# Idle matmuls over a 128-column block, and the queries of pairs 0 and 1 loaded in 1536-byte pieces

## The chip, the cores and the metric

One Trainium2 chip, one NeuronCore. The time is the device time of one execution in microseconds; the kernel before was run three times, and once more with the hardware profiler on.

## The reference

Inputs q, k, v have the shape (4 batches, 8 heads, 768 positions, 64) in float32; the output has the shape (4, 768, 512).

```python
k_chunks = k.reshape(B, H, nc, chunk, D)                    # chunks of 32 keys, nc = 24
k_min, k_max = np.min(k_chunks, axis=3), np.max(k_chunks, axis=3)
ub = np.sum(np.maximum(q[:, :, :, None, :] * k_min[:, :, None], q[:, :, :, None, :] * k_max[:, :, None]), axis=-1)
ub = np.where(causal, ub, -1e9)                             # an upper bound for each query and chunk
top_chunks = np.argsort(ub, axis=-1)[..., -6:]              # the 6 best chunks of each query
scores = scale * np.matmul(q, k.transpose(0, 1, 3, 2))      # masked: selected chunks, and not the future
attn = exp(scores - max) / (sum + 1e-9)
x = np.matmul(attn, v)                                      # heads side by side: (4, 768, 512)
h = gelu(x @ w_in); u, v = h[..., :512], h[..., 512:]       # gMLP block on the attention's output
v_n = layernorm(v) * g_ln
v_s = einsum('ts,bsd->btd', w_sg, v_n) + b_sg               # mixes positions
out = x + (u * v_s) @ w_out
```

## The kernel before

The 32 heads are worked on in 16 pairs (p, heads i = 0 and 1); pairs 0 to 3 are batch 0, and so on. For each pair:

- `load_rows` loads keys (`kn`) and queries (`qn`), one transfer for each head, and `load_v` the values. For pairs below 8 a transfer puts query 128 j + p of a head on partition p, in six pieces of 64 numbers (256 bytes).
- `kside` transposes the keys on TensorE into PSUM (`ktr`, two halves of 384 positions), takes the minimum and maximum of each chunk from there on VectorE (`kmm`, L615), and copies the keys as bf16 into `KA` (`kev`, L433 on ScalarE or L434 on VectorE). `wsub` (GpSimd, L632) subtracts the minimum from the maximum.
- `qside` transposes the queries (`qtr`): for pairs 0 to 3 in three 128x128 float32 transposes for each half of 384 positions (`rows_T`, L520; both heads at once, 64 partitions of the result each), for pairs 4 to 7 in twelve transposes of 64 rows (`rows_T2`, L530). `qev` (L433 or L434) copies each half to `qT`; `rel` makes the positive part `rT` (GpSimd L655 or VectorE L657); `qcast` makes bf16 copies `QA`.
- `select` (pairs 0 to 3) computes the bounds on TensorE (`ub`, L691) from `W`, `qT` and `rT`, and VectorE ranks them: `utr` (transpose), `m8` (nine searches for the eight largest), `dn` and `dt` (the mask `Dt`).
- `scores` computes scores into PSUM and adds the mask by matmuls (`sc`, L852 and L858); ScalarE exponentiates (`exp`, L867; L818 from pair 4 on); GpSimd cuts the diagonal; `head` multiplies by the values (`pv`, `pvd`, L890 and L897) and VectorE divides (`rcp`, `xs`).
- After a batch's four pairs, `xtrans` transposes the result (`xtr`, copied by `xev`, L434), and `moe_h` and `moe_g` compute the block: `hv` (L940), GELU and squares on ScalarE (`gv` L945, `sq` L951), `nmu` (minus the mean, L948 or L950), `rstd` (GpSimd L970), `vhat` (the normalised values: VectorE L974 or GpSimd L980), `hu` (L989) with `gu` (L994), the mixing `pt` (L1006), `vs` (L1016), `gt`, the output product `ou` (L1030) with `os` (L1039) and the stores.

`xtrans` of batch 1 ends with three copies on VectorE, and every `hv` of batch 1 waits for all four transposed tiles.

The program is a list of operations. `TABLE` was written by a planner: the order of the operations on each engine, the PSUM slot of each tile (`slots`), and which operations run on their other engine (`alt`; a `qev`, `kev` or `wbe`, for one, may run on ScalarE or VectorE). Each engine runs its list strictly in this order; an operation waits for the semaphores of what it reads and of the last user of its PSUM slot. The transfers are issued in the order of the list of SyncE (`sp`), a few by ScalarE.

PSUM has two large slots for scores (PSC) and four small ones (PSG) of one bank each for everything else.

At the start, ahead of all loads, TensorE runs matmuls whose result nobody reads (`idle`, L376): one at first, eight ahead of the first `ktr` and two ahead of the first `qtr` (`filler` in the table: `53:8 58:2`). Their operand `warm` is cleared by VectorE (L373):

```python
warm = E[1][:, 0, 0:512]
    P.op("dve", lambda d: d.memset(warm, 0.0), dve(512), ("init", 0), writes=["warm"])
    def idle(e):
        return e.matmul(ps_score.aps[1][:, 0:512], warm[:, 0:128], warm, start=True, stop=True, skip_group_check=True)
```

The helper `evac` records the copies out of PSUM: their line is L433 on ScalarE and L434 on VectorE, whatever is copied. Float32 transposes need `identF`, which GpSimd makes.

## Time and profile before

| what | us |
|---|---|
| median of three runs | 203.44 (203.07 to 204.18) |
| the profiled execution | 204.12 |
| its span, first to last instruction | 202.4 |
| mean granted TensorE clock | 0.998 of full |

Times in a view count from the start of the span. A line of the profile names a line of the kernel, the engine, the operation, and the tiles as written<-read. "xN" is a number of instructions, the figure in square brackets the idle time of the engine just before and what ended it. PE is TensorE's matmuls, PEld its weight loads, DVE VectorE, ACT ScalarE, POOL GpSimd, SPq the transfers that SyncE issues. Matmuls are pipelined: a matmul that shows 0.4 us may follow the one before it by far less, so a busy PE is not one at its peak.

### The profile page before, as it was taken

How to read it: one execution, taken by the hardware profiler on the slowest of the kernel's cores; microseconds unless marked ns; L12 is line 12 of the kernel's file. 1: busy time of each engine (PE TensorE's matmuls, PEld its weight loads, DVE VectorE, ACT ScalarE, POOL GpSimd, SP SyncE). 2: the span in 40 equal slices, each digit the busy share in tenths (PEclk: the TensorE clock that was granted, in tenths of full speed). 3: DMA queues.
4: the chain of work that ended last, by engine and by line, in shares of the span. 5: the costliest groups of instructions: out<-in, count | busy, mean ns of one | idle time of the engine just before them, and what ended most of it. 6: DMA issues, size and time to landing. Idle time of an engine off the chain costs nothing.

```text
span 202.4 us, 5906 instructions
## 1 busy us (share of the span) xinstructions
PE 192.0 (95%) x2272; PEld 122.5 (61%) x2285; DVE 170.1 (84%) x472; ACT 163.8 (81%) x278; POOL 139.7 (69%) x207
## 2 busy tenths in 40 slices
PE   7899998989999999999999999999999999998993
PEld 2556776765556665876456667764656677455642
DVE  3889999979899999999899997999698696540694
ACT  2679999999999988998989898998989986696000
POOL 6234794995798989899956998939782924067460
PEclk9999999999999999999999999999999999999999
DMA  6999999997989997988999999877972004303007
GB/s 145 221 218 197 255 236 265 329 282 184 187 185 229 161 177 118 225 206 157 179 164 181 194 221 221 185 135 110 256 132 64 4 20 123 145 13 142 3 34 277
DMA packets 113533, 34.30 MB, mean 169 GB/s; under 512 B 107233, under 2 KB 108769, under 8 KB 113506
## 3 DMA queue, kind: packets, MB, share of 16 engines
q1 hardware_dynamic: 108034, 31.80, 77.3%
q10 hardware_dynamic: 5472, 2.13, 4.5%
q8 instruction: 18, 0.29, 0.7%
q14 instruction: 9, 0.07, 0.1%
HBM read 24.38 MB, written 6.29 MB: 152 GB/s over the span
## 4 chain that ended last, share of the span: by engine, by line
PE 68%; DVE 13%; SPq 7%; DMA 6%; issue 2%; ACT 2%; POOL 0%; DVEq 0%
PE PSG L1006 12%; PE PSG L940 10%; PE PSC L812 10%; PE PSG L989 9%; PE PSG L1030 8%; PE PSG L890 5%; SPq L497 4%; DMA kn<-in_k_dram 3%; DVE W L615 3%; PE PSG L738 3%; PE PSG L520 3%; PE PSG L897 2%; PE PSG L691 2%; DVE KA L434 2%; SPq L424 2%
## 5 line engine op out<-in xcount | busy, mean ns | idle before, releaser
L818 ACT ACTIVATE E<-PSC 128x1024 bf16<-128x1024 f32 (+1 forms) x72 | 62.2, 914 | 6.2 <-PE PSC L812 5.4
L812 PE MATMUL PSC<-QA,KA 128*128 128x128 bf16 (+2 forms) x336 | 38.0, 246 | 0.2 <-ACT E L818 0.2
L1006 PE MATMUL PSG<-wsgT,vhat 128*128 128x384 bf16 x192 | 34.5, 326 | 0.5 <-ACT uT L994 0.5
L812 PEld LDWEIGHTS PSC<-QA,KA 128*128 128x128 bf16 x336 | 23.7, 98 | 10.9 <-ACT E L818 4.1
L1021 POOL TENSOR_TENSOR uT<-vgb,uT 128x384 bf16<-128x384 f32 x24 | 23.4, 982 | 6.4 <-DVE vgb L1016 6.2
L823 POOL TENSOR_SCALAR_AFFINE_SELECT E<-E 128x768 bf16<-128x768 bf16 x24 | 20.7, 872 | 9.2 <-ACT E L818 8.7
L1016 DVE SCALAR_TENSOR_TENSOR vgb<-PSG,glnT,bsgbc 128x384 f32<-128x384 f32 x32 | 18.5, 602 | 8.4 <-PE PSG L1006 8.3
L1006 PEld LDWEIGHTS PSG<-wsgT,vhat 128*128 128x128 bf16 x192 | 17.9, 98 | 12.0 <-issue 0.9
L989 PE MATMUL PSG<-xT,winb 128*128 128x384 bf16 x128 | 22.9, 326 | 0.2
L867 ACT ACTIVATE E<-PSC 128x1024 bf16<-128x1024 f32 (+1 forms) x24 | 20.8, 924 | 2.4 <-PE PSC L858 2.1
L1030 PE MATMUL PSG<-woutb,uT 128*128 128x512 bf16 (+1 forms) x91 | 21.7, 370 | 0.9 <-DVE rden L905 0.3
L940 PE MATMUL PSG<-winb,xT 128*128 128x512 bf16 x92 | 21.5, 379 | 0.8 <-issue 0.5
L890 PE MATMUL PSG<-vx,E 128*128 128x65 bf16 x480 | 19.8, 193 | 1.1 <-issue 0.5
L890 PEld LDWEIGHTS PSG<-vx,E 128*128 128x128 bf16 x480 | 17.5, 97 | 3.3 <-ACT E L818 1.0
L660 POOL CAST QA<-qT 64x768 bf16<-64x768 f32 (+1 forms) x21 | 18.7, 895 | 0.8
L989 PEld LDWEIGHTS PSG<-xT,winb 128*128 128x128 bf16 x128 | 12.0, 98 | 9.5 <-ACT uT L994 0.9
L951 ACT ACTIVATE vhat<-vgb,nmu 128x512 bf16<-128x512 f32 x24 | 17.2, 720 | 0.5 <-POOL nmu L948 0.5
L907 DVE TENSOR_TENSOR XS<-PSG,rden 128x384 bf16<-128x384 f32 x32 | 17.1, 544 | 0.5
L945 ACT ACTIVATE vgb<-PSG 128x512 f32<-128x512 f32 x24 | 14.1, 593 | 3.8 <-PE PSG L940 3.6
L994 ACT ACTIVATE uT<-PSG 128x384 bf16<-128x384 f32 x32 | 14.3, 490 | 3.0 <-PE PSG L989 3.0
L615 DVE TENSOR_REDUCE W<-PSG 128x12 f32<-128x384 f32 x32 | 16.2, 539 | 0.6 <-PE PSG L520 0.5
L940 PEld LDWEIGHTS PSG<-winb,xT 128*128 128x128 bf16 x96 | 8.9, 98 | 11.7 <-DVE xT L434 1.1
(119 smaller groups left out, 377.2 us busy)
## 6 DMA issues: line engine op xcount, KB each, us to landing
vn<-in_v_dram SPq DMA_DIRECT2D x16, 384.0 KB, 5.2
out_dram<-osb SPq DMA_DIRECT2D x14, 256.0 KB, 3.1
qn<-in_q_dram SPq DMA_DIRECT2D x31, 96.0 KB, 3.8
kn<-in_k_dram SPq DMA_DIRECT2D x15, 192.0 KB, 4.5
qn<-in_q_dram SPq DMA_DIRECT2D x15, 192.0 KB, 4.9
kn<-in_k_dram SPq DMA_DIRECT2D x29, 96.0 KB, 4.0
uT<-in_moe_w_sg_dram SPq DMA_DIRECT2D x4, 384.0 KB, 5.7
vgb<-in_moe_w_in_dram SPq DMA_DIRECT2D x3, 512.0 KB, 7.1
```

Source lines behind the costliest of these rows:

```text
L615: P.op("dve", lambda d, m=m, op=op, h=h, t=t: d.tensor_reduce(*((W[w][:, m, 0:NC].rearrange("p (j a c) -> p j a c", a=2, c=2)[:, :, h], t. ...
L660: P.op("pool", lambda g, i=i, r0=r0, r1=r1: g.tensor_copy(QA[w][i or 0][r0:r1, :], qT[r][r0:r1, :]), gps(S, 250 if i == 1 else 150), ("qca ...
L812: r = e.matmul(t.ap()[:, o:o + n], KA[w][i][:, 128 * kb:128 * kb + 128], QA[w][i][:, q0:q0 + n], start=True, stop=True)
L818: P.op("act", lambda e, t=t, c0=c0, c1=c1, i=i: e.activation(E[es][:, i, c0:c1], t.ap()[:, 0:c1 - c0], ACTF.Exp, scale=SCALE), act(c1 - c0 ...
L823: P.op("pool", lambda g, ev=ev: g.affine_select(ev, ev, pattern=[[0, NT], [1, 128]], compare_op=ALU.is_ge, fill=0.0, base=0, channel_multi ...
L867: P.op("act", lambda e, t=t, c0=c0, c1=c1, n=n: e.activation(E[es][:, :, c0:c1], t.ap().rearrange("p (i x) -> p i x", i=2)[:, :, 0:n], ACT ...
L890: r = e.matmul(t.ap()[:, 65 * qb:65 * qb + 65], E[es][:, i, a:a + 128], vx[w][:, kb, i, :], start=first, stop=False, skip_group_check=True)
L940: r = e.matmul(t.ap()[:, 0:F], xT[s][:, dk, 128 * qt:128 * qt + 128], winb[:, dk, F:DFF], start=(dk == 0), stop=(dk == NDK - 1))
L989: r = e.matmul(t.ap()[:, 0:TG], winb[:, dk, 128 * fb:128 * fb + 128], xT[s][:, dk, TG * tg:TG * tg + TG], start=(dk == 0), stop=(dk == NDK ...
L1006: r = e.matmul(t.ap()[:, 0:TG], vhat[s][:, sb, 128 * fb:128 * fb + 128], wsgT[:, sb, TG * tg:TG * tg + TG], start=(sb == 0), stop=(sb == N ...
L1021: alts=[("pool", lambda g, xg=xg, ug=ug: g.tensor_tensor(ug, xg, ug, op=ALU.mult), (860, 950), True)])
L1030: r = e.matmul(t.ap()[:, 0:c1 - c0], gT[s][:, fb, 128 * qt:128 * qt + 128], woutb[:, fb, c0:c1], start=(fb == 0), stop=(fb == NF - 1))
```

## The change

Idle matmuls: `warm` is cleared in its first 128 columns alone, and the 512 columns that stream through TensorE are those 128 read four times.

Queries of pairs 0 and 1: a transfer puts queries 6p to 6p + 5 of a head on partition p, in one piece of 1536 bytes. The transposes are made head by head: for each head twelve 64x64 transposes, from the upper and the lower 64 partitions in turn, write two PSUM tiles with a step of six columns, so that the queries come out in order. Each head so takes two PSUM slots, and four copies of 64 partitions (`qev`) take the place of two of 128 for each pair. The `qtr` of head 0 waits for the load of head 0 alone.

The tables are written anew. TensorE's list is the same but for neighbours that change places; the first `qtr` has slots 2 and 3, the second slots 1 and 3; slot 1 is used before by the first half of the keys (`ktr` 0, 0), which VectorE reads for two `kmm` and a `kev`. On VectorE's list the fourth `qev` of pair 0 comes after the four `kmm`, the `kev` and a 768-column copy into `IND`; the second `qev` of pair 1 comes after the `m8` of pair 0. The other three `qev` of either pair are on ScalarE. 75 operations change their engine. Those that VectorE runs before the last `xev` of batch 1: it gains `wbe` 0, `qev` of pairs 2, 4 and 7 (one each), `kev` of pair 3 (one), three `nmu` and one copy of 32 rows of `Dt`, and gives away `kev` of pair 2 (one), `wbe` 1, `rel` of pair 3 and one copy of `Dt`. `qcast` of pair 0 goes from ScalarE to GpSimd. All six `vhat` of batch 3 go from GpSimd to VectorE. The first transfers are: both keys of pair 0, query 0 of pair 0, `b_sg`, query 1 of pair 0, keys and queries of pair 1, one query of pair 2, and then the first 128 rows of `w_sg` (before: 22nd on the list).

```diff
--- before.py
+++ after.py
@@ -323,6 +323,7 @@
     KSPR = 8
     QL = tuple(range(8, 16))
     SPL = (4, 5, 6, 7)
+    QW = (0, 1)
     STA = tuple((b, g) for b in range(4) for g in range(2))
     GROUPS = [(0,), (1,), (2,), (3,)] + [(a, a + 1) for a in range(4, NP, 2)]
     NW = 4
@@ -370,10 +371,11 @@
     gT = uT
     osb = [T(f"osb{i}", [128, DM], F32) for i in range(3)]
 
-    P.op("dve", lambda d: d.memset(warm, 0.0), dve(512), ("init", 0), writes=["warm"])
+    P.op("dve", lambda d: d.memset(warm[:, 0:128], 0.0), (70, 180), ("init", 0), writes=["warm"])
 
     def idle(e):
-        return e.matmul(ps_score.aps[1][:, 0:512], warm[:, 0:128], warm, start=True, stop=True, skip_group_check=True)
+        return e.matmul(ps_score.aps[1][:, 0:512], warm[:, 0:128],
+                        warm[:, 0:128].rearrange("p (o x) -> p o x", o=1).to_broadcast([128, 4, 128]), start=True, stop=True, skip_group_check=True)
     P.op("pe", idle, pe(512), ("init", 1), reads=["warm"])
     P.op("pool", lambda g: g.memset(identF[:], 1.0), (77, 160), ("init", 2), writes=["identF"])
     P.op("pool", lambda g: g.affine_select(identF[:], identF[:], pattern=[[1, 128]], compare_op=ALU.is_equal, fill=0.0,
@@ -499,6 +501,13 @@
                                            bass.AP(src.tensor, (2 * p + i) * S * DH + 32 * dh, [[DH, 32], [32 * DH, NC], [1, 32]]))
                     P.op("sp", ld, dmac(), (nm, p, i, dh), writes=[(nm, s, i, dh)],
                          dma=f"{nm}{s}_{i}{dh}", xfer=600, alts=either(ld))
+            return
+        if nm == "qn" and p in QW:
+            for i in range(2):
+                def ld(e, i=i):
+                    return e.dma_start(dst[s][:].rearrange("p j i d -> p (j i d)")[:, S // 2 * i:S // 2 * i + S // 2],
+                                       bass.AP(src.tensor, (2 * p + i) * S * DH, [[NT * DH, 128], [1, NT * DH]]))
+                P.op("sp", ld, dmac(), (nm, p, i, 0), writes=[(nm, s, i, dh) for dh in range(2)], dma=f"{nm}{s}_{i}", xfer=610)
             return
         for i in range(2):
             def ld(e, i=i):
@@ -637,12 +646,28 @@
         if p in QL:
             P.op("dve", lambda d: d.transpose(qT[r][:], qn[s][:].rearrange("p j i d -> p (j i d)")), (880, 970), ("qdt", p),
                  reads=[("qn", s, i, dh) for i in range(2) for dh in range(2)],
-                 writes=[("qT", r, 0), ("qT", r, 1)])
+                 writes=[("qT", r, x) for x in range(4)])
         if p in SPL and p not in QL:
             ts = [ps_g.tile() for _ in range(2)]
             P.op("pe", rows_T2(qn[s], ts), (400, 550), ("qtr", p), mode=1,
                  reads=[("qn", s, i, dh) for i in range(2) for dh in range(2)] + ["identF"], writes=ts, alloc=tuple(ts))
-        for hf in range(2) if p not in QL else ():
+        for i in range(2) if p in QW else ():
+            ts = [ps_g.tile() for _ in range(2)]
+
+            def tr(e, i=i, ts=ts):
+                for x in range(NT):
+                    for hf in range(2):
+                        p0, c0 = 64 * hf, S // 2 * i + 64 * x
+                        last = e.matmul(ts[hf].ap()[0:64, 0:TG].rearrange("p (j x) -> p x j", x=NT)[:, x],
+                                        qn[s][:].rearrange("p j i d -> p (j i d)")[p0:p0 + 64, c0:c0 + 64],
+                                        identF[p0:p0 + 64, p0:p0 + 64], is_transpose=True)
+                return last
+            P.op("pe", tr, (400, 550), ("qtr", p, i), mode=1, reads=[("qn", s, x, dh) for x in range(i + 1) for dh in range(2)] +
+                 ["identF"] + [("qo", p)] * i, writes=ts + [("qo", p)] * (1 - i), alloc=tuple(ts))
+            for hf in range(2):
+                evac("act", lambda i=i, hf=hf: qT[r][64 * i:64 * i + 64, TG * hf:TG * hf + TG],
+                     lambda t=ts[hf]: t.ap()[0:64, 0:TG], TG, ("qev", p, i, hf), [ts[hf]], [("qT", r, 2 * i + hf)], [ts[hf]])
+        for hf in range(2) if p not in QL and p not in QW else ():
             if p in SPL:
                 t = ts[hf]
             else:
@@ -650,8 +675,8 @@
                 P.op("pe", rows_T(qn[s], t, hf), pe32(*[128] * 3), ("qtr", p, hf),
                      reads=[("qn", s, i, dh) for i in range(2) for dh in range(2)] + ["identF"], writes=[t], alloc=t)
             evac("act", lambda hf=hf: half(qT[r][:], hf) if p in SPL else qT[r][:, TG * hf:TG * hf + TG],
-                 lambda t=t: t.ap()[:, 0:TG].rearrange("p (j x) -> p j x", x=64) if p in SPL else t.ap()[:, 0:TG], TG, ("qev", p, hf), [t], [("qT", r, hf)], [t])
-        qk = [("qT", r, 0), ("qT", r, 1)]
+                 lambda t=t: t.ap()[:, 0:TG].rearrange("p (j x) -> p j x", x=64) if p in SPL else t.ap()[:, 0:TG], TG, ("qev", p, hf), [t], [("qT", r, 2 * hf), ("qT", r, 2 * hf + 1)], [t])
+        qk = [("qT", r, x) for x in range(4)]
         P.op("pool", lambda g: g.tensor_scalar(rT[r][:], qT[r][:, LO:S], 3.4028234e38, 0.0, op0=ALU.min, op1=ALU.max),
              (640, 690), ("rel", p), reads=qk, writes=[("rT", r)],
              alts=[("dve", lambda d: d.tensor_scalar(rT[r][:], qT[r][:, LO:S], 0.0, None, op0=ALU.max), dve(NSEL, rate=2), True)])
@@ -692,7 +717,7 @@
                                             tile_position=(lo, c))
             return last
         P.op("pe", ub, (1105, 1280), ("ub", pairs[0]), mode=2,
-             reads=["CMw", "CMb", "CMw1", "CMb1"] + [x for w, r in ws for x in [("qT", r, 0), ("qT", r, 1), ("rT", r)] +
+             reads=["CMw", "CMb", "CMw1", "CMb1"] + [x for w, r in ws for x in [("qT", r, 0), ("qT", r, 1), ("qT", r, 2), ("qT", r, 3), ("rT", r)] +
                     [("W", w, m, h_) for m in range(2) for h_ in range(2)]], writes=ts, alloc=tuple(ts))
         for x, t in enumerate(ts):
             for part in ((0, 128),) if x == 0 else ((0, 64), (64, 128)):
@@ -739,7 +764,7 @@
                                             stop=(m == 1), tile_position=(lo, c))
             return last
         P.op("pe", ub, (985, 1160), ("ub", pairs[0]), mode=2,
-             reads=[x for w, r in ws for x in [("qT", r, 0), ("qT", r, 1), ("rT", r)] +
+             reads=[x for w, r in ws for x in [("qT", r, 0), ("qT", r, 1), ("qT", r, 2), ("qT", r, 3), ("rT", r)] +
                     [("W", w, m, h_) for m in range(2) for h_ in range(2)]], writes=ts, alloc=tuple(ts))
         for hf, t in enumerate(ts):
             for d0, d1 in ((0, 128),) if hf == 0 else ((0, 64), (64, 128)):
@@ -1113,74 +1138,74 @@
 TABLE = {
     "pe": (
-        "1 53 49 58 60 87 83 65 92 94 31 116 99 189 191 105 109 114 197 33 239 193 160 156 195 121 199 245 165 167 247 "
+        "1 53 49 58 61 89 85 67 94 97 31 120 118 103 193 195 109 113 201 243 33 197 164 160 199 203 125 249 171 169 251 "
...
     "slots": (
-        "1310231320331200211130010323011011201021000101032303110201101021122000110102103213233003211213231200030323103320"
+        "0310231331201233201200022103102001010021320321010101312012110110103023022100101030330313003132211231111003213020"
...
```

## Rows read from the trace of the kernel before

**Rows 1.** The page's first part: engine, busy time, share of the span, instructions.
```profile
PE 192.0 (95%) x2272; PEld 122.5 (61%) x2285; DVE 170.1 (84%) x472; ACT 163.8 (81%) x278; POOL 139.7 (69%) x207
```

**Rows 2.** Windows: stretch, length, busy time of each engine, TensorE clock, DMA share, GB/s.
```profile
0.91:6.44 5.53, 4.96 (x14) 2.13 (x15) 2.73 (x7) 2.13 (x3) 3.33 (x11) 1.00 0.96 189
6.44:17.09 10.65, 9.97 (x109) 6.12 (x107) 9.90 (x40) 7.44 (x15) 2.72 (x4) 1.00 1.36 218
17.09:44.91 27.82, 26.07 (x552) 19.22 (x546) 26.18 (x78) 26.72 (x37) 21.92 (x34) 1.00 1.06 265
44.91:60.00 15.09, 14.37 (x134) 7.96 (x120) 14.02 (x47) 14.52 (x38) 11.35 (x18) 1.00 0.93 181
60.00:93.72 33.72, 32.89 (x458) 22.78 (x459) 33.41 (x97) 31.35 (x40) 31.28 (x44) 1.00 1.01 189
```

**Rows 3.** The chain that ended last, first 10 us: start, length, what.
```profile
1.88 3.58 DMA kn<-in_k_dram
5.50 1.54 PE PSG L520 x6
...
8.91 0.67 POOL rT L655
...
9.84 1.29 PE PSG L691 x18
```

**Rows 4.** The first load of keys (issued at 0.79), issue to landing; a window.
```profile
DMA to landing us min/median/max: 2.8/2.8/2.8
35.00:40.00 5.00, 4.77 (x101) 3.56 (x100) 4.48 (x12) 4.97 (x9) 4.37 (x7) 1.00 0.92 312
```

**Rows 5.** TensorE by form in three windows before 8.4 us; timeline at 52 us.
```profile
L376 PE MATMUL PSC<-E 128*128 128x512 bf16 x9 | 4.0, 631 | 1.2 <-DVE E L373 1.2
L520 PE MATMUL PSG<-identF,kn 128*128 128x128 f32 x6 | 1.5, 430 | 0.2 <-DMA kn<-in_k_dram 0.2
L520 PE MATMUL PSG<-identF,qn 128*128 128x128 f32 x6 | 0.8, 273 | 0.0
52.22 0.59 PE L530 MATMUL PSG<-identF,kn 64*128 64x64 f32 x12
```

**Rows 6.** VectorE's timeline, 0 to 17 us.
```profile
0.91 0.27 DVE L373 MEMSET E<- 128x256 uint32 x1 [0.91 <-PEq L1230]
5.10 0.65 DVE L397 COPY IND<-IND 32x768 bf16<-32x768 bf16 x1 [1.96 <-POOL IND L391]
6.44 1.20 DVE L615 TENSOR_REDUCE W<-PSG 128x12 f32<-128x384 f32 x2 [0.54 <-PE PSG L520]
...
9.07 1.95 DVE L615 TENSOR_REDUCE W<-PSG 128x12 f32<-128x384 f32 x4
```

**Rows 7.** ScalarE and VectorE by form: busy us, mean ns.
```profile
L433 ACT ACTIVATE KA<-PSG 64x384 bf16<-64x384 f32 x8 | 3.9, 484 | 0.1
L657 DVE TENSOR_SCALAR rT<-qT 128x576 f32<-128x576 f32 x3 | 2.4, 791 | 0.2
L974 DVE TENSOR_SCALAR vhat<-vgb,nmu,rstd 128x512 bf16<-128x512 f32 x9 | 4.9, 568 | 0.0
L950 DVE TENSOR_SCALAR nmu<-sm 128x1 f32<-128x1 f32 x7 | 0.9, 134 | 2.8 <-ACT vgb L945 2.8
```

**Rows 8.** Timelines of ScalarE at the first `exp`, VectorE and TensorE at 93 us.
```profile
15.64 1.02 ACT L867 ACTIVATE E<-PSC 128x1024 bf16<-128x1024 f32 x1 [1.34 <-PE PSC L858]
92.71 1.01 DVE L434 COPY xT<-PSG 128x768 bf16<-128x768 bf16 x2
93.78 1.47 PE L940 MATMUL PSG<-winb,xT 128*128 128x512 bf16 x6
```

**Rows 9.** Timelines of GpSimd and TensorE, 182 to 187 us.
```profile
182.66 0.86 POOL L970 TENSOR_TENSOR rstd<-rstd,neghalf 128x3 f32<-128x3 f32 x1
183.62 2.27 POOL L980 TENSOR_SCALAR vhat<-vgb,nmu,rstd 128x512 bf16<-128x512 f32 x3
186.04 1.14 PE L1006 MATMUL PSG<-wsgT,vhat 128*128 128x384 bf16 x6 [0.53 <-ACT uT L994]
```

More of the change, by code (lines that the diff above doesn't have):

```diff
@@ L1115 @@
     "pe": (
[13 rows of a table removed]
-    "act": (
[9 rows of a table removed]
-    "dve": (
[13 rows of a table removed]
-    "pool": (
[16 rows of a table removed]
[13 rows of a table added]
+    "act": (
[9 rows of a table added]
+    "dve": (
[14 rows of a table added]
+    "pool": (
[15 rows of a table added]
     "slots": (
-        "1310231320331200211130010323011011201021000101032303110201101021122000110102103213233003211213231200030323103320"
-        "1000101231101012013310110113000101001201101120232311000213002102201310101113011000031210111021101001202311223010"
-        "1323000310030331301301000113101110120111003110100112213322030012212120321321300231"),
+        "0310231331201233201200022103102001010021320321010101312012110110103023022100101030330313003132211231111003213020"
+        "3231110010012101010310210011000221101001031003021130323021123123333103101010100210010123010010111001011023320213"
+        "02001133211033213130102210111030101001020111001010100102212123030113310031132102030123"),
     "filler": (
```

112 rows, old and new, of the table TABLE are left out of this document.

## The prediction

> **What bounds the kernel now.** I read the page first: TensorE is busy for 192.0 of 202.4 us, VectorE for 170.1, ScalarE for 163.8, GpSimd for 139.7 [rows 1]. These are averages, so next came the windows, cut where the work changes hands. Up to 6.44 us nothing but preparation and idle matmuls runs. From 17.09 to 93.72 us VectorE stands idle for 1.64, 1.07 and 0.31 us in stretches of 27.82, 15.09 and 33.72 us; ScalarE has 1.10 us idle in the first of these, and GpSimd 2.44 in the last [rows 2]. Here three engines share the load and none has room; TensorE, 0.8 us idle in 33.7 by its modelled ends, is fed by them. At 93 us the two meet: VectorE's copies of the transposed batch 1 end at 93.72 and TensorE's `hv` begins at 93.78 [rows 8]. After that the chain of waits runs over TensorE almost alone, so a delay at 93.8 us is carried to the end, unless one of TensorE's own stalls shrinks. One such stall is large: `pt` of batch 3 begins at 186.04 after 0.53 us without a matmul. The view names ScalarE, whose copy there ends as late; but `pt` reads all six `vhat`, and GpSimd writes the last of them at 185.89 [rows 9].
>
> The front is a chain of its own: the second transfer of keys lands at 5.46, transposes begin at 5.50, and `ub` of pair 0 at 9.84 [rows 3].
>
> **The change, part by part.** *The clearing of `warm`.* It takes 0.27 us for 512 columns [rows 6]; a quarter of that is 0.07. I take 0.10, bounds 0.07 and 0.27. The first idle matmul starts at about 1.07 in place of 1.24 us. Nine of them, 0.42 us apart ((4.0 - 0.63)/8, [rows 5]), end their turn at 1.07 + 9 x 0.42 = 4.9 us. That the columns are read four times is bounded from below by no saving and, from above, by nothing that a row shows to depend on where columns lie; I take zero.
>
> *The loads.* In the front the queue moves 218 GB/s in 256-byte pieces; at 35 to 40 us, where rows of 3 and 4 KB of weights move, 312 [rows 2, 4]. A load of 196,608 bytes so takes 0.90 us, and in 1536-byte pieces between 0.63 and 0.90; I take 0.65, as the piece is nearer to the weights' rows than to 256 bytes. Four loads save 1.0 us (0 to 1.1). But the 393 KB of `w_sg`, now ahead of the second query of pair 2, take 1.3 us of the queue (393/312), so later loads arrive no earlier, and nothing past the first keys waits there for one. I cost the pieces at nothing. What pays is the order: both keys go first, so the second lands one load after the first (0.79 + 2.8 + 0.90 = 4.5 in place of 5.46, [rows 3, 4]). TensorE's turn comes at 4.9, so the first transposes begin 0.6 us earlier, and so does VectorE's first reduction (5.85 for 6.44).
>
> *Transposes of the queries.* Six 128x128 take 0.82 us for a pair (0.8, [rows 5]). Twelve of 64 rows take 0.59 us at 52 us; the new ones move as many columns. Two groups: 1.18 us, 0.36 more for each pair, 0.7 in all. If weights of 64 columns load in half the time it is 0.3; if the steps of six columns in PSUM or the half-speed clock double the time, 2.4 more. I take 0.7 and cost it at nothing: VectorE's reductions and the positive part of the queries hide it, for `ub` waits for them. Without that cover it would cost the 0.7.
>
> *Copies of the queries.* A copy of 64 partitions takes 0.48 us on ScalarE, as one of 128 does [rows 7]. Eight replace four: 2 on VectorE, 2 more on ScalarE. On VectorE copies and reductions follow each other by 0.47 us ((1.95 - 0.54)/3, [rows 6]).
>
> *The moved work.* Up to the last `xev` of batch 1, VectorE gains 2 + 5 copies out of PSUM and three `nmu`, and gives away two copies and one `rel`; the copies of `Dt` cancel. That is 5 x 0.47 + 3 x 0.13 - 0.79 = 1.95; with the overlaps of neighbouring instructions (each shows some 0.08 more than it holds the engine) 1.8 us. ScalarE loses a `qcast` of 0.83 and is otherwise even. In this stage, where VectorE has 3.0 us of idle time left [rows 2], 1.8 us cannot all be free. The front gives back 0.6, as VectorE starts sooner. Of the idle time the stretch 44.91 to 60 has 1.07, when `hv` and `hu` of batch 0 keep TensorE; I let half of it fill, 0.55. So `hv` of batch 1 comes 1.8 - 0.6 - 0.55 = 0.65 us later. Bounds: all 3.0 us fill (-1.8, limited to the -0.6 of the front, since TensorE has no shorter way), or none (+1.2).
>
> *The tail.* `rstd` ends at 183.52, and three `vhat` on GpSimd take 2.27 us [rows 9]. On VectorE one takes 0.57 us alone and some 0.5 in a row [rows 7], so 1.5. But ScalarE's list puts three `gu` ahead of its last square, which may cost up to 1.0 of its slack. Between 0 and the whole 0.53 us of the stall, I take 0.45, since each of the three saves 0.25 and the order of the `gu` has TensorE's `hu` beside it.
>
> Sum: +0.65 - 0.45 = +0.2 us. The profiled execution took 204.12 us, its span of 202.4 and 1.7 around it, and is 0.7 above the median of the runs; the sum on the median is 203.44 + 0.2 = 203.6.
>
> **The clock.** [...] The keys' transposes show 430 ns, the queries' right after the last two idle matmuls 273 [rows 5]: the clock rose between them. [...]
>
> **The rivals.** *Faster: VectorE's added work falls into its idle time.* From the point where more than 1.8 us of the 3.0 fill, the front's 0.6 is carried through: -0.6 and the stall's whole 0.53 give -1.1, 202.3 us. For it: ScalarE has a `qcast` less and VectorE's idle time sits in waits for others. Against: from 60 to 93.72 there are only 0.31 us [rows 2].
>
> *Slower: PSUM slots.* Each head's transposes take two of the four small slots. The second head needs slot 1, held by the first half of the keys until VectorE has run three `kmm` and a `kev`: 5.85 + 4 x 0.47 + 0.08 = 7.8 us. With 0.59 they end at 8.4; VectorE then still has the 0.65 us copy of `IND` and a `kmm` ahead of its `qev`, which ends at 8.4 or 7.8 + 0.65 + 0.47, the later, plus 0.5, 9.5 us. GpSimd's `rel` (0.67) waits for all four, so `ub` of pair 0 begins at 10.2 to 10.3 in place of 9.84 [rows 3]. In pair 1 the extra `qev` and `wbe` come ahead of VectorE's `rel`, another 0.5. The first `exp`, at 15.64 [rows 8], would be 1.0 us late, and ScalarE, 26.72 of 27.82 us busy after it [rows 2], would carry that into batch 0. I expect that wait to be made up: ScalarE has one copy less (0.4) and 1.1 us of idle time there. If it is not, 1.0 comes on top: +1.2, 204.6 us. It decides if `exp` of pair 3 ends over 0.6 us later than before.
>
> [...]
>
> *The pieces move no faster.* Then the four loads take 0.90 each, later loads shift by 1.0 us, and as none was waited for, the sum stays: 203.6 us.
>
> **How the numbers follow.** A difference of 0.5% (1.0 us) is about what a measurement of this kernel can tell from no change. My forecast 0.45, with its own range 202.6 to 204.4, and the pieces no faster 0.05: both within 0.5%. VectorE's idle time filled 0.25, faster. PSUM slots 0.19 and the clock 0.06, slower. So faster 0.25, within 0.5% 0.50, slower 0.25. The range has to reach both sides and leave out the outer tenth of each: from 202.2, the faster rival and a little, to 204.9, the clock's.
>
> **What would show it.** The first real transpose at 4.9 us and the first reduction at 5.85 (front right); the second `qtr` of pair 0 not before 7.8, `ub` of pair 0 after 9.84, the first `exp` later than 15.64 (slots); durations of the queries' transposes near 230 ns rather than 400 (clock); `hv` of batch 1 against 93.78 (the +0.65); the gap ahead of `pt` of batch 3 under 0.2 us, with its last `vhat` on VectorE before 185.5 plus the shift (the -0.45). The forecast is wrong if `hv` of batch 1 starts over 1 us earlier or later, or if new stalls open after 94 us, where I assume that TensorE's list costs what it did before.

## The result and the profile after

The change made the kernel slower: 205.48 us (median of five, 205.37 to 205.93) against 204.12 (five runs beside it, 203.07 to 204.18), ratio 1.0101 with a 95% interval of 1.0077 to 1.0124. 203.6 was predicted, in a range up to 204.9. The profiled execution took 205.37 us (span 203.6) against 204.12 (span 202.4). In four further comparisons the kernel before had medians of 203.52 to 203.86 over 23 to 35 runs: its profiled execution is itself 0.3 to 0.6 above what it usually takes. A few executions below took over 1.5% longer than the fastest of their kernel; they count in the medians and not in the ratios.

The page's first part, after, beside [rows 1]: VectorE gained 6.3 us of work, GpSimd lost 6.9.

```profile
PE 192.1 (94%) x2321; PEld 121.9 (60%) x2321; DVE 176.4 (87%) x489; ACT 162.2 (80%) x276; POOL 132.8 (65%) x197
```

The windows after, cut as in [rows 2] (start and end, length, busy time of PE, PEld, DVE, ACT, POOL, clock, DMA share, GB/s): VectorE starts earlier (3.06 us of work before 6.44, where it had 2.73), and has 0.95 us idle in the fourth stretch, where it had 1.07.

```profile
0.91:6.44 5.53, 5.37 (x29) 2.35 (x29) 3.06 (x11) 2.57 (x4) 3.19 (x11) 1.00 0.84 211
...
44.91:60.00 15.09, 13.84 (x116) 7.71 (x115) 14.14 (x49) 13.84 (x37) 9.46 (x15) 1.00 1.03 208
60.00:93.72 33.72, 32.72 (x465) 23.00 (x463) 33.42 (x96) 30.63 (x39) 31.53 (x44) 1.00 0.99 164
```

The front after, TensorE's timeline (start, length, line, what, idle time ahead and its releaser), beside [rows 3, 5]: the keys' transposes begin at 4.75 and not at 5.50, the second head of pair 0 waits 0.83 us for a reduction, and the bounds (L716) begin at 9.63 for pair 0 (9.84 before) and at 13.67 for pair 1 (13.41 before).

```profile
1.04 3.68 PE L377 MATMUL PSC<-E 128*128 128x512 bf16 x9 [1.04 <-DVE E L374]
4.75 0.88 PE L529 MATMUL PSG<-identF,kn 128*128 128x128 f32 x6
...
5.99 0.53 PE L661 MATMUL PSG<-identF,qn 64*64 64x64 f32 x12
7.34 0.53 PE L661 MATMUL PSG<-identF,qn 64*64 64x64 f32 x12 [0.83 <-DVE W L624]
...
9.63 0.69 PE L716 MATMUL PSG<-qT,W 64*32 64x288 f32 x8 [0.64 <-POOL rT L680]
```

VectorE's timeline there, beside [rows 6]: the memset takes 0.11, the first reduction begins at 5.34 (6.44 before), and the copy of queries stands behind the fourth reduction.

```profile
0.88 0.11 DVE L374 MEMSET E<- 128x64 uint32 x1 [0.88 <-PEq L1255]
...
5.34 1.02 DVE L624 TENSOR_REDUCE W<-PSG 128x12 f32<-128x384 f32 x2 [2.22 <-PE PSG L529]
...
7.68 0.56 DVE L624 TENSOR_REDUCE W<-PSG 128x12 f32<-128x384 f32 x1
8.27 0.55 DVE L436 COPY qT<-PSG 64x384 f32<-64x384 f32 x1
```

At 94 us `hv` of batch 1 begins 0.37 us later than in [rows 8].

```profile
94.15 3.19 PE L965 MATMUL PSG<-winb,xT 128*128 128x512 bf16 x14
```

The tail is where the two differ most. ScalarE's timeline after: behind the last exponential (169.63) it stands idle for 4.70 us, waits for VectorE's `gt` (L1044), and only then loads the table for the GELU.

```profile
165.69 3.94 ACT L843 ACTIVATE E<-PSC 128x640 bf16<-128x640 f32 x5 [0.37 <-PE PSC L837]
174.33 1.28 ACT L970 ACT_TABLE_LOAD   x1 [4.70 <-DVE uT L1044]
175.63 0.60 ACT L970 ACTIVATE vgb<-PSG 128x512 f32<-128x512 f32 x1
```

In the kernel before, the same load ran in the idle time, and the first GELU then waited for TensorE alone:

```profile
165.25 3.94 ACT L818 ACTIVATE E<-PSC 128x640 bf16<-128x640 f32 x5 [0.68 <-PE PSC L812]
169.21 1.28 ACT L945 ACT_TABLE_LOAD   x1
173.45 0.60 ACT L945 ACTIVATE vgb<-PSG 128x512 f32<-128x512 f32 x1 [2.96 <-PE PSG L940]
```

The chain that ended last, after (start, length, what), confirms it. Before, it ran over TensorE here, but for one ScalarE copy of 0.50 us at 185.56. Now it goes from VectorE over ScalarE's table load, its GELUs and squares, GpSimd's power and VectorE's `vhat` to `pt` at 187.31 (186.04 in [rows 9]).

```profile
173.70 0.57 DVE uT L1044
174.27 0.02 issue
174.29 0.02 ACTq L204
174.30 0.03 issue
174.33 1.28 ACT L970
...
184.91 0.87 POOL rstd L995
185.77 0.03 issue
185.80 1.47 DVE vhat L999 x3
187.27 0.04 issue
187.31 7.97 PE PSG L1031 x48
```

Three marks are used below, each the end of one instruction: the mask `dt` of pair 1 (17.09 before, 17.34 after), the last copy of transposes, `xev` of batch 3 (172.22, 172.67), and the last sum of the output (199.84, 201.12). The **tail** from the second to the third took 27.62 us before and 28.45 after.

### The profile page after: what moved, and what is told of

Read it like the earlier page. It is cut to its first block, busy times and chain, and to the rows that moved or that the text cites. A ratio compares the mean times of both kernels' runs of the same rounds, so it can differ in the third digit from the quotient of the medians.

```text
span 203.6 us, 5989 instructions
## 1 busy us (share of the span) xinstructions
PE 192.1 (94%) x2321; PEld 121.9 (60%) x2321; DVE 176.4 (87%) x489; ACT 162.2 (80%) x276; POOL 132.8 (65%) x197
## 4 chain that ended last, share of the span: by engine, by line
PE 59%; DVE 19%; ACT 17%; issue 2%; POOL 1%; DVEq 0%; ACTq 0%
PE PSG L1031 11%; PE PSC L837 11%; PE PSG L1055 8%; PE PSG L915 6%; PE PSG L1014 5%; ACT E L892 5%; ACT vgb L970 4%; ACT vhat L976 3%; PE PSG L965 3%; ACT E L843 3%; DVE W L624 3%; PE PSG L716 2%; PE PSG L763 2%; PE PSG L922 2%; PE PSC L377 2%
## 5 line engine op out<-in xcount | busy, mean ns | idle before, releaser
L837 PE MATMUL PSC<-QA,KA 128*128 128x128 bf16 (+2 forms) x336 | 37.3, 246 | 0.4 <-ACT E L843 0.2
L1046 POOL TENSOR_TENSOR uT<-vgb,uT 128x384 bf16<-128x384 f32 x23 | 21.2, 925 | 8.2 <-DVE vgb L1041 7.7
L1031 PEld LDWEIGHTS PSG<-wsgT,vhat 128*128 128x128 bf16 x192 | 17.9, 98 | 11.8 <-DVE vhat L999 0.9
L1055 PE MATMUL PSG<-woutb,uT 128*128 128x512 bf16 (+1 forms) x100 | 23.7, 371 | 0.3 <-ACT vgb L970 0.3
L965 PE MATMUL PSG<-winb,xT 128*128 128x512 bf16 x96 | 22.2, 380 | 0.0
L685 POOL CAST QA<-qT 64x768 bf16<-64x768 f32 (+1 forms) x20 | 17.8, 893 | 0.9 <-POOL vhat L1005 0.2
L932 DVE TENSOR_TENSOR XS<-PSG,rden 128x384 bf16<-128x384 f32 x32 | 17.1, 546 | 0.5
L680 POOL TENSOR_SCALAR rT<-qT 128x576 f32<-128x576 f32 x14 | 9.4, 676 | 9.6 <-DVE qT L436 7.5
```

Of the source, the lines that this page charges most:

```text
L837: r = e.matmul(t.ap()[:, o:o + n], KA[w][i][:, 128 * kb:128 * kb + 128], QA[w][i][:, q0:q0 + n], start=True, stop=True)
L965: r = e.matmul(t.ap()[:, 0:F], xT[s][:, dk, 128 * qt:128 * qt + 128], winb[:, dk, F:DFF], start=(dk == 0), stop=(dk == NDK - 1))
L1031: r = e.matmul(t.ap()[:, 0:TG], vhat[s][:, sb, 128 * fb:128 * fb + 128], wsgT[:, sb, TG * tg:TG * tg + TG], start=(sb == 0), stop=(sb == N ...
L1046: alts=[("pool", lambda g, xg=xg, ug=ug: g.tensor_tensor(ug, xg, ug, op=ALU.mult), (860, 950), True)])
L1055: r = e.matmul(t.ap()[:, 0:c1 - c0], gT[s][:, fb, 128 * qt:128 * qt + 128], woutb[:, fb, c0:c1], start=(fb == 0), stop=(fb == NF - 1))
```

## The experiments

Ratios are to the kernel before, run on the same chip in the same hours, with 95% intervals.

| kernel | median us | before | ratio | tail us |
|---|---|---|---|---|
| changed, again | 205.94 | 203.58 | 1.0101 (1.0070 to 1.0132) | 28.46 |
| changed, early GELU | 204.71 | 203.52 | 1.0042 (1.0010 to 1.0075) | 27.19 |
| changed, other buffer | 204.80 | 203.79 | 1.0058 (1.0018 to 1.0098) | 26.97 |
| changed, tail of before | 204.76 | 203.52 | 1.0057 (1.0031 to 1.0083) | 27.49 |
| before, changed tail | 204.90 | 203.52 | 1.0074 (1.0044 to 1.0105) | 28.57 |
| before, changed front | 204.62 | 203.58 | 1.0065 (1.0034 to 1.0095) | 27.61 |
| changed front, old idle | 204.74 | 203.86 | 1.0026 (0.9994 to 1.0059) | 27.62 |
| before, new idle | 203.41 | 203.52 | 0.9991 (0.9962 to 1.0021) | 27.55 |
| changed, score buffer and GELU | 205.40 | 203.58 | 1.0068 (1.0034 to 1.0101) | 27.18 |
| changed, wide copies | 207.91 | 203.86 | 1.0218 (1.0169 to 1.0266) | 28.46 |
| changed, copies on ScalarE | 205.93 | 203.79 | 1.0109 (1.0075 to 1.0144) | 28.45 |
| changed, middle back | 206.19 | 203.86 | 1.0109 (1.0059 to 1.0159) | 28.46 |
| changed, buffer and middle | 204.01 | 203.79 | 1.0004 (0.9970 to 1.0038) | 26.96 |
| before, new idle, new tail, GELU | 203.27 | 203.58 | 0.9971 (0.9942 to 1.0000) | 27.17 |
| before, new idle, new tail, other buffer | 204.25 | 203.79 | 0.9987 (0.9947 to 1.0027) | 26.98 |
| wide front, new tail, GELU | 205.15 | 203.86 | 1.0055 (1.0023 to 1.0087) | 27.17 |

The tail's length is the same within 0.15 us wherever the tail is the same; the same front differs by up to 0.9 from run to run (the mask of pair 1 ends between 17.02 and 17.93). So the traces settle the tail better than the times do.

**The table load in time.** A GELU of six columns on ScalarE behind the last exponential:

```diff
+    gl = T("gl", [128, NT], F32)
+    P.op("act", lambda e: e.activation(gl[:], neghalf[:], ACTF.Gelu_apprx_tanh), act(6), ("gl", 0), reads=["neghalf"],
+         writes=["gl"], table="gelu")
```

> The changed kernel, with one tiny GELU on ScalarE right behind its last exponential, so that the 1.28 us table load runs in ScalarE's 4.70 us of idle time and not behind its wait for gt_2_1_2. Theory (the load behind the wait is the loss of the tail): gv_3_0 starts at about 174.3 instead of 175.63, the last square ends 1.3 earlier, and the time is 205.48 - 1.28 = 204.2 (203.9 to 204.5), a ratio to the kernel before of about 1.000. Rival (VectorE's work of the middle is the loss, ScalarE only passes it on): 205.3 to 205.5, ratio 1.006 to 1.007. Second rival (ScalarE's list with five GELUs ahead of the last square is the loss): part of the 1.3 is given back at the last squares, 204.6 to 205.0.

The tail took 27.19 us, 1.26 less; the ratio fell from 1.0101 to 1.0042. ScalarE's timeline: the load runs at 170.34, and the first GELU starts right behind `gt`, without it.

```profile
170.34 1.28 ACT L1137 ACT_TABLE_LOAD   x1
171.64 0.21 ACT L1137 ACTIVATE gl<-neghalf 128x6 f32<-128x6 f32 x1
175.04 0.60 ACT L970 ACTIVATE vgb<-PSG 128x512 f32<-128x512 f32 x1 [3.19 <-DVE uT L1044]
```

The load behind the wait is shown as the tail's loss. The time, 204.71, is above the range expected and lies in that of the second rival; but from the first GELU to the end of the last square it takes 8.83 us with the edit and without, so nothing of the 1.26 was given back there. The kernel is still slower than before: the tail is not all.

**Halves exchanged.** The lists, engines and slots from the last exponential on are taken from the other kernel, in both directions; the code stays.

> The changed kernel up to the last exponential, then the lists, engines and PSUM slots that the kernel before had for the rest (batch 3 behind its attention, vhat on GpSimd again). Theory (tail): the lateness of the middle alone stays, +0.45 at the last piece of XS, so 204.12 + 0.45 = 204.6 (204.3 to 204.9), ratio 1.002. Rival (middle): the tail is innocent, the time stays at 205.2 to 205.6.

> The kernel before up to the last exponential, then the changed kernel's lists, engines and slots for the rest. Theory (tail): the tail's own loss without the front and the middle, 1.29 at the end less 0.45 at 172, so 204.12 + 0.84 = 205.0 (204.7 to 205.3), ratio 1.004; ScalarE's table load stands behind a wait for gt_2_1_2 of VectorE. Rival (middle): 204.0 to 204.3, no loss.

Neither theory held alone. Both times lie in the ranges expected, but those were counted from 204.12, and the kernel before took 203.52 here: with the old tail 1.24 us stay (204.76 - 203.52), where 0.45 was expected; with the new tail alone 1.38 come, where 0.84 was. Each half loses, by 0.6 and 0.7%.

**The idle change alone.**

```diff
-    P.op("dve", lambda d: d.memset(warm, 0.0), dve(512), ("init", 0), writes=["warm"])
+    P.op("dve", lambda d: d.memset(warm[:, 0:128], 0.0), (70, 180), ("init", 0), writes=["warm"])
-        return e.matmul(ps_score.aps[1][:, 0:512], warm[:, 0:128], warm, start=True, stop=True, skip_group_check=True)
+        return e.matmul(ps_score.aps[1][:, 0:512], warm[:, 0:128],
+                        warm[:, 0:128].rearrange("p (o x) -> p o x", o=1).to_broadcast([128, 4, 128]), start=True, stop=True, skip_group_check=True)
```

> The kernel before with the short memset and the idle matmuls' operand read four times over, and nothing else. The prediction's step for the front: first reduction 0.6 earlier, at 5.85; by the changed kernel's trace up to 1.1, at 5.3. Theory: the lead is spent at the first wait for loaded queries, 203.8 to 204.2, no difference at the end. Rival (a lead at the front is kept to the end): 203.0 to 203.5. Second rival (the operand read four times over keeps TensorE's clock lower or slows the idle matmuls): 204.5 and more.

No difference at the end: 203.41 lies in the first rival's range, but the kernel before took 203.52 beside it. The mask of pair 1 was done at 16.32, 0.77 earlier than before, and the kernel stayed ahead until 83 us. There GpSimd waits 2.22 us for values, where it waited 0.42 before, and by 92 us the lead is gone. The kernel before, then this one:

```profile
85.80 1.11 POOL L428 CAST vx<-vn 128x768 bf16<-128x768 f32 x1 [0.42 <-DMA vn<-in_v_dram]
...
86.21 0.83 POOL L429 CAST vx<-vn 128x768 bf16<-128x768 f32 x1 [2.22 <-DMA vn<-in_v_dram]
```

**The changed kernel again, and its front alone.** The second takes the changed kernel's lists up to the bounds of pair 1, and from the first scores on those of before.

> The changed kernel once more, as it is, so that the three others of this chip have it beside them. Its trace is to say what its front usually does: the first trace had the first key transposes at full clock (0.88 us for six) and the first block bounds at 9.63; two kernels with the same front had 1.48 and the bounds at 10.21 and 10.1. Theory of three shares (front +0.6 to +0.8, middle +0.45, tail +0.84): 1.9 to 2.1 over the kernel before, ratio 1.009 to 1.010. Rival (tail and middle alone): +1.3, ratio 1.006.

> The changed kernel's front, with short memset, idle operand, pieces and half transposes, in its own order up to the bounds of pair 1, and from the first scores on the lists, engines and slots of the kernel before (its tail too). Theory (the front is a share of the loss): bounds of pair 0 at about 10.1 and first exponential at 15.9 to 16.1, against 15.3 to 15.6 in three traces with the old loads, so +0.6 to +0.8 in time, ratio 1.003 to 1.004. Rival (a front's difference is taken up by later waits for transfers, as the lead of the idle change was): within 0.3, ratio 0.999 to 1.0015.

The front alone costs 1.04 us in the medians (ratio 1.0065), more than the 0.6 to 0.8 expected. In the trace of the changed kernel's second run the six transposes of keys took 1.49 us, where the first had 0.88 for the same instructions. Six such transposes took about as long, 1.48 us, in another run, where the profile's clock column showed 0.55 (last runs below); here it shows 1.00. The bounds of pair 0 then begin at 10.21:

```profile
1.04 4.02 PE L377 MATMUL PSC<-E 128*128 128x512 bf16 x9 [1.04 <-DVE E L374]
4.85 1.49 PE L529 MATMUL PSG<-identF,kn 128*128 128x128 f32 x6
...
7.92 0.53 PE L661 MATMUL PSG<-identF,qn 64*64 64x64 f32 x12 [0.68 <-DVE W L624]
...
10.21 0.69 PE L716 MATMUL PSG<-qT,W 64*32 64x288 f32 x8 [0.64 <-POOL rT L680]
```

So the first trace had caught a favourable front. With the old loads the mask of pair 1 was done between 16.3 and 17.1 (four traces; a fifth, of the kernel with the old front and the other buffer, has 18.29, after 0.75 us of waiting for the keys and with 1.49 us for the first queries' transposes in place of 0.82), with the new ones between 17.0 and 17.9 (eight).

**The front with the old idle.**

> The kernel with the changed front and the rest of before, but with the old memset and the old idle operand: the pieces, half transposes and their lists by themselves. Theory (pieces cost, idle change gives a little): the idle matmuls start 0.2 later, first reduction up to 0.5 later, 0.0 to 0.4 over the kernel with the changed front and new idle (whose ratio was 1.0065), so 1.0065 to 1.0085. Rival (the operand read four times over is what costs, in the clock): 1.000 to 1.003.

The ratio, 1.0026, lies in the rival's range, and its interval ends at 1.0059, below the theory's. The trace says the opposite: the mask of pair 1 comes at 18.13, 0.2 behind that of the new idle, and the bounds at 10.42. The idle change alone cost nothing either (0.9991). So the loss is put on the pieces and their transposes by the traces, while the times leave open how large it is: 0.9 us in these medians, 1.04 in the others.

**Why the front is late.** The chain that ended last goes through VectorE's queue in the changed kernel: from the first reduction over a copy of the keys, two more reductions and the copy of `IND` between them to VectorE's copy of the queries, then over `rel` to the bounds. Its last steps in the first trace:

```profile
7.68 0.56 DVE W L624
...
8.27 0.56 DVE qT L436
...
8.91 0.68 POOL rT L680
...
9.63 1.29 PE PSG L716 x18
```

Three edits try the causes. The first, beside the early GELU, gives the second head of pair 0 a free buffer of the scores (a part of the edit):

```diff
-            ts = [ps_g.tile() for _ in range(2)]
+            wide = (p, i) == (0, 1)
+            ts = [ps_score.tile()] * 2 if wide else [ps_g.tile() for _ in range(2)]
+            at = [512 * hf * wide for hf in range(2)]
...
```

> The changed kernel with the early GELU, and the second head of pair 0 transposed into a scores' PSUM buffer that is free until the first scores, so that it waits for no reduction; its copy on VectorE stands ahead of the last reduction of pair 0. Theory (the wait for a PSUM slot and VectorE's queue behind it set the bounds of pair 0): second head's transposes 0.5 to 0.8 earlier, bounds at 9.7 to 9.8, then limited by the weights' reductions; 0.4 off the early GELU's time, so 1.0 to 1.2 under the changed kernel's own of this chip for GELU, and 1.4 to 1.6 for both: ratio to the kernel before 1.002. Rival (VectorE's eight reductions are the bound, the slot is not): bounds still at 10.1, time as with the early GELU alone, ratio 1.004.

The transposes no longer waited (7.31), but as both copies read one tile, VectorE's copy now waited for ScalarE's, with a reduction behind it: bounds at 11.15, and 1.0068, above both expectations. It tells nothing of the slot by itself. The second moves VectorE's two copies of queries to ScalarE (a line of the table):

> The changed kernel with the two query copies that VectorE has in the front (one for each pair) on ScalarE instead. Theory A (VectorE's queue of reductions and copies sets the front): the reductions of pair 1 come 0.5 earlier, bounds of pair 0 at 9.9 to 10.1, of pair 1 0.4 to 0.6 earlier than 14.24, end -0.4. Theory B (the wait for a PSUM slot sets it): bounds of pair 0 at 10.1 to 10.3 and of pair 1 at 14.1 to 14.4, no gain.

No gain, as theory B has it. In a run with short transposes of the keys (0.82 us) the second head still waited 0.83, and the bounds began at 9.56 and 13.62, against 9.63 and 13.67 in the first trace of the changed kernel. But that does not make the slot the one cause. With VectorE's copy away the chain goes from the third reduction over the second head's transposes and ScalarE's copies, and `rel` begins at 8.84, where it began at 8.91: the two ways to it are equally long.

```profile
7.33 0.55 PE PSG L661 x12
...
7.90 0.87 ACT qT L435 x2
...
8.84 0.68 POOL rT L680
```

The third puts both heads into one pair of slots with two copies of 128 partitions (the lines of the transposes):

```diff
-                        last = e.matmul(ts[hf].ap()[0:64, 0:TG].rearrange("p (j x) -> p x j", x=NT)[:, x],
+                        last = e.matmul(ts[hf].ap()[64 * i:64 * i + 64, 0:TG].rearrange("p (j x) -> p x j", x=NT)[:, x],
                                         qn[s][:].rearrange("p j i d -> p (j i d)")[p0:p0 + 64, c0:c0 + 64],
-                                        identF[p0:p0 + 64, p0:p0 + 64], is_transpose=True)
+                                        identF[p0:p0 + 64, p0:p0 + 64], start=True, stop=True, skip_group_check=True, tile_position=(p0, 64 * i))
```

> The changed kernel, with one change in its front: both heads of a pair go into the same two PSUM slots (the second head by ordinary matmuls with the identity into partitions 64 to 127), so that a pair needs two slots and two copies of 128x384, both on ScalarE, and not four slots and four copies of 64x384 over ScalarE and VectorE. Theory (slots and doubled copies make the front late): no wait for a reduction ahead of the second head, bounds of pair 0 at 9.2 to 9.5 instead of 10.21, two copies of 0.55 less on VectorE, time 0.7 to 1.0 under the changed kernel: ratio 1.005 to 1.006. Rival (the front is late because two key loads ahead of the queries make it so, or because of VectorE's eight reductions): bounds at 10.0 to 10.2, ratio 1.009 to 1.010.

The wait for a reduction was gone and the bounds of pair 0 began at 9.75, where two changed kernels with keys' transposes as short (1.2 us) have 10.04; `rel` now stood behind the fourth reduction and `wsub`. But the bounds of pair 1 came at 14.74 (14.24 before the edit): TensorE waited 0.59 us for the one pair of copies ahead of `wbm` (L483, which spreads `b_sg` over the partitions), and the 24 ordinary matmuls of a pair took 1.44 us, where the transposes took 1.16. Another 1.0 us was lost between 42 and 49 us, of which the trace shows 0.36 as time in which TensorE had no instruction. Why it lost 2 us in the median stays open. So the front has several ways of nearly the same length, and no edit of one of them gave its loss back.

```profile
6.38 1.44 PE L661 MATMUL PSG<-identF,qn 64*64 64x64 f32 x48
...
9.75 0.69 PE L717 MATMUL PSG<-qT,W 64*32 64x288 f32 x8 [0.46 <-POOL rT L681]
...
13.10 0.91 PE L483 MATMUL PSG<-bsgbc,onesr 1*128 1x384 f32 x2 [0.59 <-ACT qT L435]
```

**The middle.** Five instructions of batch 0, 1.27 us, go from VectorE back to GpSimd and ScalarE.

> The changed kernel with five instructions of batch 0 taken off VectorE again and put where the kernel before had them (three nmu and one qd on GpSimd, one copy of queries 7 on ScalarE): 1.27 us of VectorE's time between 47 and 84. Theory (VectorE is the bound there, the +0.45 of the middle is its added work): the stretch from gv_0_0 to exp_6_0_0, 37.01 and 37.00 in two traces against 36.57, comes down to 36.5 to 36.7, the time by 0.3 to 0.5. Rival (another engine or the order of lists sets it): 36.9 to 37.1.

In the trace the stretch took 36.49 us, 0.5 less, as the theory has it; a gap of 0.66 us that TensorE has at 57.45 in the changed kernel's second run, and in every trace with these lists, is gone. The view names no releaser for that gap; by the program the transposes behind it wait for VectorE's copy of the keys of pair 7, which ends at 58.01, 0.1 ahead of them. The time did not show the gain (1.0109, four runs). Nor is 36.57 a firm mark: the kernel with the front alone has before's lists here and takes 35.98.

**The other buffer.** `gv` of block 0 waited for `gt` only because `gt` reads the buffer that it overwrites:

```diff
-                kx = k % NT if b < B - 1 else (0, 1, 2, 3, 3, 4, 5, 3)[k]
+                kx = k % NT if b < B - 2 else ((0, 1, 2, 3, 4, 5, 2, 1), (0, 1, 2, 3, 3, 4, 5, 3))[b - B + 2][k]
```

> The changed kernel with one index changed: the product of batch 2's seventh block stands in the third buffer of vgb and not in the first, so that gv_3_0 waits for TensorE alone, and not for gt_2_1_2 too. No GELU is added. Theory (a second wait in front of gv_3_0 holds the table load as well): the load goes into ScalarE's idle time by itself and gv_3_0 starts as soon as TensorE has its block, 0.4 to 0.6 ahead of the early-GELU kernel: 1.6 to 1.9 off the tail, ratio to the kernel before 1.001 to 1.003. Rival (the load stands wherever its first GELU stands): -0.4 to -0.6 alone, ratio 1.007.

> The kernel before with the short memset, the idle operand, the changed tail and the other buffer, no GELU added. Theory: tail from the last transposes to the end 26.6 to 26.9 (27.6 before, 27.2 with the early GELU), time 0.7 to 1.0 under the kernel before, ratio 0.995 to 0.9965. Rival: 27.2 and 0.997, as with the early GELU.

The tail took 26.97 and 26.98 us: 1.48 off, 0.2 more than with the early GELU, less than the 1.6 expected. The times show no gain over the early GELU (1.0058 and 0.9987, both above the ranges expected, which the intervals just reach). In the trace of the first the load moved into the idle time by itself:

```profile
169.88 1.28 ACT L970 ACT_TABLE_LOAD   x1
174.08 0.60 ACT L970 ACTIVATE vgb<-PSG 128x512 f32<-128x512 f32 x1 [2.92 <-PE PSG L965]
```

**Added up.**

> The changed kernel with the other buffer and with the five instructions of batch 0 taken off VectorE again. Theory of three shares: tail -1.6 to -1.9, middle -0.5, only the front (+0.6) is left against the kernel before, less the tail's gain of 0.7: ratio 0.998 to 1.002. Rival (shares overlap): 1.004 and more.

204.01 us, ratio 1.0004: mended in the tail and the middle, the changed kernel cannot be told from the kernel before (0.9970 to 1.0038). Here, however, the stretch of the middle took 37.18 us, not 36.49, with a wait of 0.5 for VectorE's `wsgT` in place of the other. So the share of the middle is not settled by these two runs.

**The version that the runs pointed to.**

> The kernel before with only what the runs so far speak for: the short memset and idle operand, old query loads, the changed kernel's tail (vhat of batch 3 on VectorE), and the early GELU. Theory: from the last transposes to the end 27.2 instead of 27.6, as in the early-GELU trace, so -0.4 in time, with the idle change nothing more: ratio 0.997 to 0.999. Rival (the tail of after is worse even without the table load's wait): 1.001 and more.

> What the runs so far speak for together: the changed front with two wide copies for each pair, the kernel before from the first scores to the last exponential, the early GELU and the changed tail. Theory: bounds of pair 0 at 9.2 to 9.5 (before 9.84), so -0.3 to -0.6 at the front, -0.4 at the tail, 0 in the middle: 0.7 to 1.0 under the kernel before, ratio 0.995 to 0.9965. Rival (the lead of the front is given back at waits for transfers): -0.4 alone, ratio 0.998.

The first took 203.27 us, ratio 0.9971, at the edge of what can be told from 1; its tail is 0.45 shorter than before. The wide front took the second to 1.0055, far from what was expected; in its trace six transposes at 14.02 took 1.48 us with a granted clock of 0.55 (0.992 over the whole execution), behind waits of TensorE of 1.13, 0.54 and 0.59 us in 6 us, and the mask of pair 1 came at 20.13.

## Why the prediction was wrong

Two terms of the sum failed: the tail, which has the wrong sign, and the new front, which was costed at nothing. A third came out right by luck.

**The front.** "First transposes at 4.9, first reduction at 5.85": measured 4.75 and 5.34, and 4.85 and 5.74 in the second run; right. That the transposes and the slots would cost nothing was wrong: the front alone costs 1.04 us in the medians, and about 0.9 by the mask of pair 1. The rival "PSUM slots" had the place right: the second head waits for the third reduction, VectorE's copy of the queries comes behind the fourth, and the bounds of pair 0 begin at 10.21 in the second run (10.2 to 10.3 was its figure; 9.63 in the first). Its first exponential, 16.6, came at 15.47 and 16.05 (16.47 with the front alone). Its test was whether the exponentials of pair 3 end over 0.6 us later than before (40.04). They end at 39.82 and 40.39 in the changed kernel and at 41.12 with the front alone: by that mark the wait was made up behind the changed lists, as the prediction expected, and not behind the old ones.

**The clock.** The forecast gives 0.06 to a clock that stays low through the queries of both pairs and ends its range, at 204.9, with it. No run shows that term: behind two idle matmuls the queries' transposes took 220 ns each in the first trace (1.1 us for 24) and 0.53 us for each twelve in the second. The pace did differ from run to run, but at the keys: 0.88 or 1.49 us for six, with idle matmuls ahead of both. What sets it there no run shows.

**The moved work.** "+0.65 at `hv` of batch 1": 94.15 against 93.78, +0.37 in the first trace, 94.71 and +0.93 in the second, whose front is 0.57 later. The size is right, but by luck: 0.65 was a gain of 0.6 from the front and a loss of 1.25 from the moved work. With the front alone, and the lists of before behind it, `hv` begins at 94.31, so the front gave nothing back but cost 0.5, and the moved work added 0.4 (both traces have the bounds of pair 0 at 10.21). The front alone, then the changed kernel's second run:

```profile
94.31 1.04 PE L965 MATMUL PSG<-winb,xT 128*128 128x512 bf16 x4
...
94.71 1.04 PE L965 MATMUL PSG<-winb,xT 128*128 128x512 bf16 x4
```

Up to 93.72 us VectorE was busy for 87.3 us after (all five windows) and for 86.2 before [rows 2]: 1.1 us of added work went into its idle time, where the sum let 0.55 go there.

**The tail** is the step that failed most: -0.45 was forecast, +0.84 measured (28.45 - 27.62). Its own mechanism was right: with the load out of the way the same tail takes 27.17 to 27.19, 0.43 to 0.45 less than before. What I saw and mispriced was ScalarE: I counted the `gu` ahead of its last square, which add 0.5 (the last square ends 8.83 us after the first GELU's start, before 8.29), and took the first GELU's start as given. It started 2.18 us later, 175.63 against 173.45: 0.45 because the last copy of transposes ends that much later, 1.28 from the table load and the remaining 0.45 from the wait for `gt`, of which another buffer gave back 0.2. The prediction's last sentence named the case ("if new stalls open after 94 us"), but gave it no chance of its own.

**The sum** with what was measured, on the median of before: front +1.0, middle +0.4, tail +0.8 is 2.2; 2.36 was measured in the second run (205.94 - 203.58). The forecast was +0.2. The tail's share is shown by its traces; front and middle are each no larger than what one comparison can tell from nothing (intervals of 0.6 us to either side), and how the two divide stays open. The profiled execution of before hid part of the front: it took 204.12 us, with 0.49 us at 41.56 in which TensorE had no instruction and for which the view names no releaser. Three other traces with the old front have no such stall; a fourth has 0.85 us there, and of the thirteen with a new front three have 0.36 to 1.12 us between 34 and 46 us. What causes them is open.

```profile
41.56 0.49 PE L890 MATMUL PSG<-vx,E 128*128 128x65 bf16 x11 [0.49 <-issue]
```

## What to carry to other kernels

When an order of instructions changes, look at what each engine's list does first in a new phase, and at every wait of that first instruction: a buffer that is overwritten counts as a wait, and a table load (1.28 us here) can end up behind it. A lead at the front was worth something here only up to the next wait for a transfer. Two terms of a sum can be wrong and cancel at one mark, so each wants a run of its own. And a single profiled execution should be placed among its runs before a difference of half a microsecond is read from it.

## What the runs showed of the hardware

**Where the table load stands.** With one wait on the first GELU (TensorE's) the load ran ahead of it, in idle time: at 169.21 before, and at 169.88 in the changed kernel with the other buffer, 4.20 us or more ahead of the GELU. With two waits, the second as an instruction of its own (`ACTq L204`, at 174.29), it ran behind that, at 174.33. The load took 1.28 us each time; the one at 169.21 starts 0.02 us behind the last exponential, and the GELU at 175.63 0.02 us behind its load.

**Copies beside GpSimd's work.** VectorE's copy of `KA` (L811) took 0.35 us where GpSimd was idle (at 46.81 us), and 0.85 where a GpSimd instruction had, by the estimate below, begun just before it. VectorE and GpSimd of the changed kernel's second run:

```profile
46.81 0.35 DVE L811 COPY KA<-kb 64x768 bf16<-64x768 bf16 x1
...
56.01 0.85 DVE L811 COPY KA<-kb 64x768 bf16<-64x768 bf16 x1
55.13 2.37 POOL L1005 TENSOR_SCALAR vhat<-vgb,nmu,rstd 128x512 bf16<-128x512 f32 x3
```

The mean of the eight copies rose from 371 ns before to 464, by two of them (0.70 and 0.85; the others take 0.34 to 0.39). If each of the three `vhat` has a third of the 2.37 us (an estimate), the second begins at 55.92, 0.09 us ahead of the copy, and ends at 56.71, 0.15 ahead of the copy's end. With the middle moved back the copy began at 55.82, also beside three `vhat` (55.00 to 57.49), at about the start of the second by the same estimate (55.83), and took 0.35. So where a GpSimd instruction begins beside such a copy went with how long it took, though the copy itself was not moved; what holds it up no run shows.

**The pace of the first matmuls.** The same nine idle matmuls took 3.46, 3.68, 3.91 and 4.02 us in four traces of the changed kernel and its variants; the profile's clock column shows 1.00 over the nine that took 3.68. At 4.02, and with the 0.63 us that one shows in [rows 5], they follow each other by 0.42 us, (4.02 - 0.63)/8; the fourteen matmuls of the same shape at 94.15 us, `hv`, which show 0.38 each, follow each other by 0.22, (3.19 - 0.38)/13. Where the nine took less, some of them followed faster, so the pace rose among them, and otherwise behind them. With that, and with transposes of the keys that began between 4.43 and 4.85 us, the bounds of pair 0 moved between 9.30 and 10.21.
